# A planned mLSTM and top-1 expert kernel: paced row stores, two joined lead tiles, a shorter selection and a new order

## The chip, the cores and the metric

The kernel runs on one core of one Trainium2 chip. The metric is device time in microseconds of one execution, and the time of a kernel is the median of its runs.

## The reference, cut to what matters

An mLSTM recurrence over 768 steps, for 4 batches and 8 heads of width 40, gives 3072 tokens of 320 numbers. Each token goes to the one expert of eight that its gate picks, and the expert's two-layer product is scaled by the gate's probability.

```python
for t in range(S):                                   # B, H, S, D = 4, 8, 768, 40
    m_new = np.maximum(f_gate[:, :, t] + m, i_gate[:, :, t])
    f_stab, i_stab = np.exp(f_gate[:, :, t] + m - m_new), np.exp(i_gate[:, :, t] - m_new)
    C = f_stab * C + i_stab * einsum('bhd,bhe->bhde', vt, kt)
    n = f_stab * n + i_stab * kt
    y[:, :, t] = sigmoid(o_gate) * einsum('bhde,bhe->bhd', C, qt) / max(abs(n . qt), 1)
...
x = y.transpose(0, 2, 1, 3).reshape(3072, 320)
logits = x @ w_gate + modality_bias[modality_id]     # 8 experts
e_idx = argmax(logits); gate_w = softmax(logits)[e_idx]
for e in range(8):
    out[e_idx == e] = gate_w * (maximum(x @ w1[e], 0) @ w2[e])   # w1 320x1024, w2 1024x320
```

## The kernel before, in words

**What runs.** `still_arm` (from L1654) is the arm that these inputs take. It treats the recurrence's state as settled after the first 64 steps of each batch, so a chunk of 128 tokens is one set of products of queries with a state (`light`, L1955; `light16`, L1979; `special`, L2070). There are 24 chunks. `token_rows` (L1996) divides, gates and splits two chunks at a time into 16-bit rows in the tile `rows`; the dividing multiply of a pair of chunks runs on GpSimd (L2027), the split on ScalarE (L2029) and VectorE (L2031).

**From chunks to expert tiles.** Tokens are sorted by modality, because with this bias almost all tokens of a modality choose the same expert: class A and class B. Each chunk's 128 rows are stored to their sorted places in the DRAM tensor `x_s` by an indirect transfer that GpSimd issues (`scatter_rows`, L2035). Two transfers of `prefill` (L2050, issued on SyncE by L2054 and L2055) first fill parts of `x_s` with empty rows, and every row store waits for them. SyncE fetches an expert tile of 256 rows back, transposed, once the chunks that can hold its rows have landed (`load_tile`, L2120). The first three tiles of class A do not go through DRAM: `select` (L2142) multiplies rows of a chunk by a 0/1 matrix and so gets the transposed tile in PSUM. These lead tiles are A0 with 128 rows, from chunks 0 to 2; A1 with 64 rows, from chunks 1 to 3; and A2 with 128 rows, from chunks 2 to 5. Each chunk of a selection is five matmuls (L2158), two half ones (L2161) and two products of one column each (L2163) that bring the token's number in two parts into one PSUM column.

**The expert.** `expert` (L2221) first forms the hidden layer of a tile, eight blocks of 128 hidden units, each from six full matmuls (L2255) and from half-height ones for the last 64 inputs (L2263). ScalarE applies the ReLU (L2243), VectorE forms the remainder (L2244), and 24 matmuls for each 128 rows give the output (L2295). A part of 64 rows does them in pairs. ScalarE scales the output (L2310) and GpSimd scatters it to `out` (L2311).

**What sets the order.** Nothing is issued in the order of the source. Every piece of work is a task with an engine, a duration and what it reads and writes. `Plan.run` (L65) is a list scheduler: of the tasks that are ready on an engine it takes the one with the least latest time plus a nudge, one letter of the string `PRIO` for each task, (character code − 79) × 0.5. Each transfer has a second letter, in `LOADS`, which shifts by the same rule the moment from which it may be planned; the letters stand in the order in which the transfers are declared, and those of `prefill` are the 14th and 15th. The instructions are then written to each engine's queue in the order of the planned starts, and each engine works through its queue in order. For each gap of TensorE in the plan's first 60, `emit` (L2485) puts in idle matmuls on zeros (L2494).

**Limits around GpSimd.** `swdma` (L1680) makes every GpSimd transfer wait for the completion of the last but one before it. `Plan.run` keeps tasks marked `port` from overlapping, since GpSimd and some VectorE operations share a port.

Of the kernel before, what the change touches and what calls it, by code (L numbers as in the profile page):

```python
# [21 lines left out]
class Plan:  # L22
# [151 lines left out]
P = 128  # L174
# [42 lines left out]
def kernel(  # L217
# [1346 lines left out]
LEAD = {"A0": (0, 3), "A1": (1, 4), "A2": (2, 6)}  # L1564
STREAM = ["A0", "A1", "A2", "B0", "B1", "A3", "B2", "A4", "B3", "A5", "B4", "A6", "B5", "A7"]
# [6 lines left out]
    "+i&.3%&&nIL8]tk*G%<-YU4cr2-I{Q]G'%E)%g+%Q%3dK`7M_D%p%%R22j%SS;J05Cj+-]I{&K*)99Lz{n%{f[Ut%)^OI&UT{2f'(R2lf-KAaB"  # L1572
    "22%=%vwLleYz]{%N-,B8CBT%{%0/(%k>+%qM%T^[8(%i,%,t5OAt4;h@/{T.%>,t'=+m>@dSV4i@91)^/%l,&%DfAmT&*L;P5(B%%%+sO&Z0Ez"
    "{nc_pkYo%A)\\vk8T]M5)Zy]EEq\\y{%P*/KZ2JV%/QhvP9GRL3>/-bPCSSa%QL9>.jW)JI,-2lkA{+%5-Q4=&_>%{%';J%MrK-K,%gnRmh/-/^%"
    "%%B%%+(VXI',s:'4.%/g%S%0=9'r9\\SG%9-EPfl{Y4w]DB\\&8Q+s%W7^,Sr%dWl/%mkW@>%%%%%%(9F?(V(%Tkhk\\{YHP*n_5v23ep&%1cl=HU"
    "n%bV]%MjlD'[e%\\4*%%&%,E?(@%x*\\Ts'N0.{\\Wsy'{;/qif{.Qod48%%{*%qD5k,R,UBn9'\\c1'KEr))%\\@(%d%%%%?(,&%%)%[/VWns5<Z[D"
    "euy[_s{@X26)uk?Is'O/.W%>aH%%%1n?J'mr/'7?)<'E^6-%%*%%,B%%%%8%F7(x-<*dCmC%[dZCD4P5v+2&-@GE%+@t%RL.-&'%.r%7)\\g/']"
    "^%@''S/'%%;%%%E(11%%%%7)*4'007W{Q%dw2bFX;M:bFR%Q2,t7m%Rx:@1%.%g%0'Ur/,'j/C'6rB?%%,%%%H05.%%1%@OO4%vUs<*HcIM'\\z"
    "bN*neWM/)M2B)BP{/Y%ip%-L:7k6-BJRI)HY1%/%83b.ns%K'D_22%0%%%%uF%%%%%%:AUb<4=<{\\%cai\\^VP,4%+/(*`/%h%g,+]%/6?%%%8<"
    "M(2%D:%%;(C{QxNtE3H'1?S[%x<03V@92+{{'hh)*8{1_%%6:,%F5^l&lSKmKD7kiTs/{xAt6%W'46Yr0%GB0'oli1'c\\3&%%%1%/\\(%%*%%0A"  # L1580
    ",9HN*6%7'%c/Q%R:M'kO3'%%%%%&A(B'%%%%M(',vrt@'tL.'H[JS%;:=+%%%'B%?(&%:%)%;93(K&@r/F_T7,rRrb'R%/'%%%%%%D(%%%%%%5"
# [63 lines left out]
def still_arm(tc, a, out):  # L1645
# [10 lines left out]
    def pe(dur, fn, r=(), w=(), **k):  # L1656
        plan.add("PE", dur, fn, r, w, **k)
# [32 lines left out]
    sws = []  # L1690
# [345 lines left out]
    def scatter_rows(c):  # L2036
        def scatter():
# [9 lines left out]
    scats = {}  # L2047
# [589 lines left out]
```

## Time and profile before

| what | value |
| --- | --- |
| median of 3 runs | 223.42 us (222.77, 223.42, 224.87) |
| the profiled execution's own time | 225.65 us |
| span of the profiled execution | 223.8 us, so 1.85 us lie around it |
| TensorE busy | 212.5 us, 95% of the span |
| VectorE, ScalarE, GpSimd busy | 139.0, 99.2, 75.6 us |
| mean granted TensorE clock | 0.986 of full speed |
| DMA | 30.77 MB, mean 137 GB/s |

The busy time of TensorE contains the idle matmuls on zeros and whatever ran at a lower clock, so a busy TensorE is not the same as useful work. The parts of the page that matter most here are the slices of the span, where the granted clock and the DMA share stand under each other, and the chain of work that ended last, which goes through TensorE for most of its length.

### The profile page before, as it was taken

Reading aid. Unit: us, or ns where it says so; the run is one execution under the profiler, and the core shown is the slowest. Engines: PE = TensorE matmul, PEld = TensorE weight load, DVE = VectorE, ACT = ScalarE, POOL = GpSimd, SP = SyncE. Lnnn points to the kernel's source line nnn. Section 1 sums busy time; section 2 is a strip of 40 time slices with the busy share of each in tenths; the row PEclk is TensorE's granted clock in tenths of the full one; section 3 lists DMA queues with packets and bytes.
Section 4 is the critical chain, followed back from the end, with each engine's and each line's share of the span. In section 5 each row is a group of like instructions: output and inputs, shape, how many; then the busy total and the mean of one; then the engine's idle time right before and its main releaser. Section 6 shows DMA issues by size and latency. Waiting matters only on the chain.

```text
span 223.8 us, 5532 instructions
## 1 busy us (share of the span) xinstructions
PE 212.5 (95%) x2180; PEld 160.6 (72%) x2182; DVE 139.0 (62%) x446; ACT 99.2 (44%) x202; POOL 75.6 (34%) x84
## 2 busy tenths in 40 slices
PE   8998997999999999899999999999999999999790
PEld 3665785897877777677777787777777877777550
DVE  7987765469795895989428149346831770449800
ACT  2497766385645814774336033234235321313220
POOL 5122228224535264552452126552511103111031
PEclk9999999699999999999999999999999999999997
DMA  6999879457262621755414410240191100691010
GB/s 190 357 309 398 288 203 305 186 127 253 80 166 93 146 106 61 191 150 90 149 59 104 152 62 0 106 113 11 62 237 14 46 3 29 153 378 62 3 39 21
DMA packets 27115, 30.77 MB, mean 137 GB/s; under 512 B 19190, under 2 KB 19480, under 8 KB 26824
## 3 DMA queue, kind: packets, MB, share of 16 engines
q1 hardware_dynamic: 24520, 22.06, 33.2%
q0 software_dynamic: 2416, 8.13, 10.7%
q8 instruction: 19, 0.31, 0.6%
q10 hardware_dynamic: 144, 0.13, 0.2%
q14 instruction: 16, 0.13, 0.2%
HBM read 18.57 MB, written 8.22 MB: 120 GB/s over the span
## 4 chain that ended last, share of the span: by engine, by line
PE 65%; issue 18%; DMA 5%; DVE 4%; POOL 3%; SPq 1%; POOLq 1%; ACT 0%; ACTq 0%
PE O L2295 24%; PE H L2255 21%; PE H L2263 6%; PE M L2494 3%; DMA qg<-in_ql 3%; PE Y L1969 3%; POOL out L2311 3%; DMA out<-ob,ois 2%; SPq L1941 1%; PE M L2195 1%; PE Y L2094 1%; PE Y L2079 1%; PE O L2158 1%; DVE ql L1977 1%; DVE hl L2244 1%
## 5 line engine op out<-in xcount | busy, mean ns | idle before, releaser
L2244 DVE SCALAR_TENSOR_TENSOR hl<-H,hh 128x512 f16<-128x512 f32 (+1 forms) x52 | 33.6, 656 | 29.8 <-ACT hh L2243 25.9
L2243 ACT ACTIVATE hh<-H 128x512 f16<-128x512 f32 (+1 forms) x52 | 29.4, 571 | 51.4 <-PE H L2263 30.9
L2295 PEld LDWEIGHTS <-hh 128*128 128x128 f16 (+1 forms) x400 | 38.4, 99 | 14.4 <-ACT w2hB L1942 0.2
L2311 POOL DMA_INDIRECT out<-ob,ois x25 | 25.5, 1019 | 66.8 <-ACT ob L2310 36.6
L2255 PE MATMUL H<-xt,w1hA 128*128 128x256 f16 (+2 forms) x256 | 36.3, 252 | 0.9 <-issue 0.9
L2038 POOL DMA_INDIRECT x_s<-rows,pos_i x24 | 24.1, 1006 | 32.0 <-DVE hl L2244 7.9
L2255 PE MATMUL H<-xt,w1hB 128*128 128x256 f16 x192 | 32.9, 273 | 0.0
L2255 PE MATMUL H<-xt,w1lA 128*128 128x256 f16 (+2 forms) x128 | 29.9, 252 | 0.5 <-issue 0.5
L2310 ACT ACTIVATE ob<-O,zs 128x320 f32<-128x320 f32 x24 | 12.5, 525 | 38.2 <-PE O L2295 19.9
L2295 PE MATMUL O<-w2hA,hh 128*128 128x320 f16 (+1 forms) x104 | 28.1, 304 | 0.0
L2295 PE MATMUL O<-w2lA,hh 128*128 128x320 f16 (+1 forms) x104 | 28.1, 304 | 0.0
L2295 PE MATMUL O<-w2lB,hh 128*128 128x320 f16 x96 | 26.4, 299 | 0.0
L2295 PE MATMUL O<-w2hB,hh 128*128 128x320 f16 x96 | 26.4, 299 | 0.0
L2255 PE MATMUL H<-xt,w1lB 128*128 128x256 f16 x96 | 26.2, 272 | 0.0
L2255 PEld LDWEIGHTS <-w1hA 128*128 128x128 f16 x256 | 21.0, 99 | 6.0 <-issue 3.7
L2295 PEld LDWEIGHTS <-hl 128*128 128x128 f16 (+1 forms) x200 | 19.2, 98 | 7.9 <-issue 0.5
L2027 POOL TENSOR_TENSOR xr<-xr,ab 128x640 f32<-128x640 f32 x11 | 14.9, 1358 | 25.7 <-DVE ab L2010 19.9
L2255 PEld LDWEIGHTS <-w1hB 128*128 128x128 f16 x192 | 17.4, 98 | 4.2 <-issue 2.1
L2295 PE MATMUL O<-w2hA,hl 128*128 128x320 f16 (+1 forms) x104 | 15.9, 299 | 0.0
L2012 DVE SCALAR_TENSOR_TENSOR xr<-og,Y 128x320 f32<-128x320 f32 x24 | 11.3, 477 | 7.3 <-PE Y L2094 4.9
L2295 PE MATMUL O<-w2hB,hl 128*128 128x320 f16 x96 | 15.0, 299 | 0.0
L2494 PE MATMUL M<-zz 128*128 128x512 bf16 (+7 forms) x46 | 12.9, 427 | 1.3 <-DVE zz L1785 1.1
(205 smaller groups left out, 344.0 us busy)
## 6 DMA issues: line engine op xcount, KB each, us to landing
qg<-in_ql SPq DMA_DIRECT2D x11, 384.0 KB
og<-in_ogl SPq DMA_DIRECT2D x12, 320.0 KB
stage<-in_w1s SPq DMA_DIRECT2D x8, 320.0 KB
stage<-in_w SPq DMA_DIRECT2D x8, 320.0 KB
stage<-in_w1t SPq DMA_DIRECT2D x1, 1280.0 KB
og<-in_w SPq DMA_DIRECT2D x1, 1280.0 KB
kvs<-in_kvs SPq DMA_DIRECT2D x2, 364.5 KB
sp<-in_spq SPq DMA_DIRECT2D x4, 160.0 KB
```

The costliest lines, as they stand in the source:

```text
L1969: t_.matmul(y[p0:p1, HQ * g:HQ * g + w], lhsT=q[0:k, i, g, p0:p1], rhs=Ss[b][0:k, g, 0:w], start=(g == 0), stop=(g == 2), skip_group_check ...
L2012: dve(320, lambda h=h: v.scalar_tensor_tensor(x4[:, h], og[k][:, h].rearrange("p (h d) -> p h d", h=H), 1.0, y4[h][:, :, 0:D], ALU.add, AL ...
L2027: pool(640, lambda: g_.tensor_tensor(x3, x3, ab.rearrange("p c h o -> p (c h) o").broadcast_to([P, 2 * H, D]), ALU.mult), r=abk, w=xk)
L2038: ins = g_.indirect_dma_start(out=x_s[:, :], out_offset=bass.IndirectOffsetOnAxis(ap=pos_i[:, c:c + 1].bitcast(U32), axis=0), in_=rows[:, ...
L2243: act(g * n, lambda: s_.activation(hh[:, sl, 0:n], hp3, AF.Relu), r=[nb], w=[f"hh{j}{i}" for i in fs])
L2244: dve(g * n, lambda: v.scalar_tensor_tensor(hl[:, sl, 0:n], hp3, 0.0, hh[:, sl, 0:n], ALU.max, ALU.subtract), r=[nb] + [f"hh{j}{i}" for i ...
L2255: t_.matmul(dst, lhsT=w[:, i, ws], rhs=x[:, xb], start=(first and b == 0 and q == 0), stop=(last and b == 1 and q == 2), skip_group_check= ...
L2263: t_.matmul(dst, lhsT=w[rs, place(f)[0], 2 * T:WP], rhs=x[rs, xs[r]], start=(first and r == 1 and m == 0 and q == 0), stop=(m == len(pairs ...
L2295: t_.matmul(op[p0:p0 + nr, 0:DM], lhsT=t[:, at[f], P * h:P * h + nr], rhs=w[:, f], start=(i < ways), stop=(i >= 24 - ways), skip_group_che ...
L2310: act(400, lambda op=op, o=o, qc=qc, nr=nr: s_.mul(obs[o][0:nr], op[0:nr, 0:DM], facs[0:nr, qc:qc + 1]), r=[no, f"fac{k}"], w=[f"ob{o}"])
L2311: swdma(164, lambda o=o, qc=qc, nr=nr: disjoint("outf", g_.indirect_dma_start(out=out[:, :], out_offset=bass.IndirectOffsetOnAxis(ap=ois[0 ...
L2494: t_.matmul(bank[b][:, 0:m], lhsT=zz, rhs=zz[:, 0:1].broadcast_to([P, m]), start=True, stop=True, skip_group_check=True)
```

## The change

Four things change together.

1. GpSimd's transfers no longer wait for the last but one before them. In the plan, any GpSimd transfer that would start before `UNTIL` is moved to at least `GAP` after the one before. In the program, a chunk's row store that the plan starts before `UNTIL` waits for the last VectorE instruction that the plan has ended by then.
2. Tiles A1 and A2 get one buffer, side by side, and one pass through `expert`: the hidden layer of 192 columns at once, then the output of the 64 rows and of the 128 rows.
3. A chunk of a selection brings both parts of the token's number by one matmul of two columns; VectorE adds the two when it copies them.
4. `PRIO` and `LOADS` are new strings (`PRIO`, eleven lines of letters, is left out below).

```diff
+    GAP = 2.4
+    UNTIL = 48.0
...
+        last_sw = -100.0
...
             if t["port"]:
                 s = max(s, port_free)
+                if t["kb"] is not None:
+                    s = max(s, last_sw + self.GAP) if s < self.UNTIL else s
+                    last_sw = s
                 port_free = s + t["dur"]
...
+JOINT = ("A1", "A2")
...
 LOADS = (
-    "7%D.4%V6%%K7{t{0^+cV]6:%3n^>{{b)>4RR;I2+,{Clb%4{q.%00QeG/'g+0i@={7du*T%B%y?8FY(B9..'fSaVV+/MH{&%?Bf5((D%Df%Z,["
+    '(1%@7KO:%.5-{jlT=%.%,M%CeJOgFm&tuM%IN3`uGP1G<+{W0GN%+Dh%8{2nLGa%Su7c_%zC2b7%,DH)ZX4Jy<I0UKIn%^%@B=2NfjjcHge<1I'
...
     def swdma(kb, fn, r=(), w=(), **k):
-        def go():
-            ins = fn()
-            if len(sws) > 1:
-                tc.add_manual_dep(ins.ins, sws[-2].ins.name, mybir.DependencyInfo(mybir.DependencyClass.Sync, mybir.DependencyReason.DATA),
-                                  reason="two of GpSimd's transfers under way")
-            sws.append(ins)
-
-        plan.add("POOL", 1.05, go, r, w, kb=kb, port=True, **k)
+        plan.add("POOL", 1.05, fn, r, w, kb=kb, port=True, **k)
...
             scats[c] = ins
+            if pace:
+                tc.add_manual_dep(ins.ins, pace[-1].ins.name, mybir.DependencyInfo(mybir.DependencyClass.Sync, mybir.DependencyReason.DATA),
+                                  reason="transfers of rows follow one another at the plan's distance")
...
+        if name in JOINT:
+            at = TILES[name][0] - TILES[JOINT[0]][0]
+            j0, nj = STREAM.index(JOINT[0]) % SLOTS, sum(TILES[m][1] for m in JOINT)
+            whole = xt[j0][:, 0:6 * nj].rearrange("p (b n) -> p b n", b=6)
+            x = whole[:, :, at:at + n]
...
-                for w in range(2):
-                    t_.matmul(o1[0:n, ib:ib + 1], lhsT=sel, rhs=tok2[:, c, w:w + 1], start=False, stop=z_ and w == 1, skip_group_check=True)
+                t_.matmul(o1[0:n, ib:ib + 2], lhsT=sel, rhs=tok2[:, c], start=False, stop=z_, skip_group_check=True)
...
-            dve(1, lambda: v.tensor_copy(ids[0:n, q:q + 1], o1[0:n, ib:ib + 1]), r=[n1_, "ids_z"], w=[f"ids{k}"])
+            dve(2, lambda: v.tensor_scalar(ids[0:n, q:q + 1], o1[0:n, ib:ib + 1], o1[0:n, ib + 1:ib + 2], None, ALU.add), r=[n1_, "ids_z"], w=[f"ids{k}"])
...
     def expert(k):
         s = slots[k]
+        if s["name"] in JOINT[1:]:
+            return
+        subs = [m for m in range(len(STREAM)) if STREAM[m] in JOINT] if s["name"] in JOINT else [k]
+        c, n, x = s["cls"], s.get("nj", s["n"]), s.get("whole", s["x"])
...
-        sets = [(0, 1), (2, 3), (4, 5), (6, 7)] if n == T or by_piece else [(0, 1, 4, 5), (2, 3, 6, 7)]
+        sets = [(0, 1), (2, 3), (4, 5), (6, 7)] if n > P or by_piece else [(0, 1, 4, 5), (2, 3, 6, 7)]
...
+        t = plan.tasks[i]
+        pace.clear()
+        if t["w"] and t["w"][0][:2] == "xs" and plan.start[i] < plan.UNTIL:
+            pace.extend([max((z, n, x) for n, (z, x) in enumerate(steps) if z <= plan.start[i])[2]])
+        made = t["fn"]()
+        if t["eng"] == "DVE" and hasattr(made, "ins"):
+            steps.append((plan.end[i], made))
```

## Rows read from the trace of the kernel before

**Rows 1.** The page, busy time of each engine, share of the span, instructions

```profile
PE 212.5 (95%) x2180; PEld 160.6 (72%) x2182; DVE 139.0 (62%) x446; ACT 99.2 (44%) x202; POOL 75.6 (34%) x84
```

**Rows 2.** Idle matmuls of L2494 by stretch: us, PE and weight loads busy, clock, DMA, GB/s

```profile
0.00:24.00 24.00, 14.16 (x51) 5.11 (x53) 1.00 0.91 319
```

**Rows 3.** Timeline of PE: start, length, what, and the idle time before it

```profile
21.34 0.87 PE L1969 MATMUL Y<-S,qg 120*128 120x123 f32 x6 [0.55 <-DMA qg<-in_ql]
```

**Rows 4.** The chain of waits, in order of time: start, length, what

```profile
37.01 0.53 PE H L2255 x18
37.54 0.39 issue
...
38.15 0.52 issue
...
38.86 0.52 issue
...
39.63 0.46 PE H L2263 x24
```

**Rows 5.** Stretches: us, busy PE, PEld, DVE, ACT, POOL (instructions), clock, DMA, GB/s

```profile
38.00:39.00 1.00, 0.34 (x3) 0.06 (x3) 0.00 (x0) 0.00 (x0) 0.98 (x2) 1.00 0.99 397
...
40.00:50.00 10.00, 10.00 (x156) 8.88 (x150) 6.45 (x22) 6.36 (x14) 1.86 (x2) 0.83 0.48 135
```

**Rows 6.** Timeline of POOL: the first and the fifth row store

```profile
32.14 1.18 POOL L2038 DMA_INDIRECT x_s<-rows,pos_i  x1 [4.84 <-DVE w1lB L1943]
...
37.46 0.97 POOL L2038 DMA_INDIRECT x_s<-rows,pos_i  x1 [0.30 <-issue]
```

**Rows 7.** The page, the DMA queue of instructions with most packets: packets, MB, share

```profile
q8 instruction: 19, 0.31, 0.6%
```

**Rows 8.** The line of the number products, all instructions: ns min, median, max

```profile
L2163 PE MATMUL O<-cst,sel x20: 163/170/178, 14.6 to 32.5; 128*128 128x1 f16 x14, 128*64 128x1 f16 x6
```

**Rows 9.** The chain of waits at number products and an idle matmul

```profile
22.80 0.80 PE M L2494 x4
...
28.52 0.13 PE O L2163 x2
```

**Rows 10.** The chain of waits at hidden layers, of 128 and then of 256 columns

```profile
45.14 1.45 PE H L2255 x24
46.59 0.78 PE H L2263 x24
...
68.61 1.31 PE H L2255 x12
69.92 0.76 PE H L2263 x12
```

**Rows 11.** What POOL waited for: us in total, times, longest

```profile
POOL x_s L2038 <- DMA out<-ob,ois: 3.2, 2, 2.7
```

**Rows 12.** Timeline of SyncE's queue: filler rows of `x_s`, B0's load

```profile
18.51 0.98 SPq L2054 DMA_DIRECT2D x_s<-zrow  x1
...
28.39 0.61 SPq L2055 DMA_DIRECT2D x_s<-zrow  x1
...
43.61 1.46 SPq L2126 DMA_TRANSPOSE xt<-x_s  x1
```

**Rows 13.** Stretches: DMA share ahead of the row stores and behind B0's load

```profile
28.00:32.00 4.00, 4.00 (x58) 3.45 (x55) 3.50 (x9) 2.20 (x4) 0.00 (x0) 1.00 0.63 154
...
47.00:48.00 1.00, 1.00 (x23) 0.90 (x18) 0.89 (x2) 0.66 (x3) 0.00 (x0) 1.00 0.66 259
48.00:49.00 1.00, 1.00 (x18) 1.00 (x17) 0.97 (x2) 1.00 (x2) 0.24 (x1) 1.00 0.09 27
```

**Rows 14.** Timeline of PE: B0's first matmuls

```profile
54.07 0.38 PE L2255 MATMUL H<-xt,w1hB 128*128 128x256 f16 x2
```

**Rows 15.** Timeline of DVE and of ACT: rows of chunks 4, 5 and A2's last copy

```profile
28.57 0.88 DVE L2031 TENSOR_TENSOR rows<-xr,rows 128x128 f16<-128x128 f32 x2
...
35.38 0.37 ACT L2172 CAST xt<-O 128x256 f16<-128x256 f32 x1
```

**Rows 16.** Timeline of POOL: the last output store

```profile
218.74 0.97 POOL L2311 DMA_INDIRECT out<-ob,ois  x1 [1.83 <-ACT ob L2310]
```

More of the change, by code (lines that the diff above doesn't have):

```diff
@@ L1571 @@
 PRIO = (
[L1572 to L1581, printed above, removed]
@@ L1582 @@
-    "(,%xjr>'CCD'pMO:-R>))+A%%%R7%%3*%%%_("
+    "{r&(,%u6*7PG+X<;_Zu]mk{3Z{3,&d'.-4-+2{{utsf0/KK%%@%Sm75{zg%(\\bj5hg1^eRl7K\\_JHTRSQ'fKMs+;7%s{{P4+WLGnKREzPNM{[P"
+    "Z%T5s.1(aVd[SUN{D9*3+&/*+PvUHV8LM;{%&ENRM;63)oW%%%'*;D.ZUrHNW_Npt-%fW_RQ_?xOe_K%.Z4Q3O+Rs.73E2N%1[\\X_[WO*5eSAq"
+    'L1PYU6P%?%5fi4gsDyWJIF8M{7^IH`Wp&%r()50A%%(%4%=4%%k{OOk9/%Z%/%;0>??1ITWGcy{U%VZ[fSGDGHswuS40.10HP2SmwqDBn.P,Qd'
+    '`y][t;FX%u(&%2%(%%0%%8T-%)%%BA>2HJ=6L[@c?)%{;%WVEC%+946[EXzzxT\\WzWXzswQOY]F^mtpoxmq_@%kXlidH{%Y%r%%%<):@MC&MMY'
@@ new lines @@
+    "Vzi%'BMfwGQE-?vCs{,YT%%%%%{X?3zpur{bo_{{z%{%[yoIEz%DiiLTdt{urZw]imwTm_fu\\OdbbRRYRtsr<xLKIFE`%/%%%+%9QHfsyoz{1Q"
+    "Nzm3yI>UT^VQJ2%NE{rt{QjI`y'fp`dc`]aM+oy.)l2'xD%x\\YroW=Eq{r%)B%%c[{w{h\\{{W{mnE5WXUeSE/(KHEASPnQjWyh4@m4HEEaPIBy"
+    "=>@M<:x/310**(d3I%%%J{&%I_dd`^K`{{z@J%*%')%F''%%%uuP/(L6Qk.3Md1*jKEh+{b'F30:8o%-,)(&:E,+I%+*{pvk-PB{],o{_`4Vsq"
+    "OS]jSyH{O*{,-wcceH^Qc=U`yHv'4P6yq,jJ:R7,_7MGs2IVT>V,&MC8PNSg%%Q%fehW@a4e%*%f1C7PMwL1JnqAGEWNIGjLD2)'%';3%'03%0"
+    "0%+Q.+cce)%et_cbq%%A?uvtsNv*Qh{O:1(U'm]C%DvI]9>DC@@zs00-fd,*naXQTg%%<(*+ET0+6&*7bAJ4*:y7'%@(9*%D%B?24\\c-%5E3:{"
@@ L1583 @@
+    "y*1N`),2sk0+K]3%-&'%ZE%*%@%%0>[i@''\\dCIKY,4.,B<*RS,))%><3%.%97.'*%%%/:7M;`J8,&,5'0*5*,&.%*%3;*.9975*(*%%)+KI5["
+    "G1,&/,@0.+',&/-'%(%%',%%%))2%"
 )
 LOADS = (
-    "7%D.4%V6%%K7{t{0^+cV]6:%3n^>{{b)>4RR;I2+,{Clb%4{q.%00QeG/'g+0i@={7du*T%B%y?8FY(B9..'fSaVV+/MH{&%?Bf5((D%Df%Z,["
-    '?2X\\k%)4]%VLN{,`[-y@'
+    '(1%@7KO:%.5-{jlT=%.%,M%CeJOgFm&tuM%IN3`uGP1G<+{W0GN%+Dh%8{2nLGa%Su7c_%zC2b7%,DH)ZX4Jy<I0UKIn%^%@B=2NfjjcHge<1I'
+    'AjB%%/5NT4L:DC]X{6%W'
 )
@@ L2105, in tile_rows @@
         hs = halves(name)
-        slots[k] = dict(name=name, cls=name[0], n=n, hs=hs, nh=len(hs), r0=r0, need=need, x=xt[j][:, 0:6 * n].rearrange("p (b n) -> p b n", b=6), s=j,
-                        q=slice(hs[0][0], hs[0][0] + len(hs)))
+        x = xt[j][:, 0:6 * n].rearrange("p (b n) -> p b n", b=6)
+        if name in JOINT:
[3 more added lines that the diff above has]
+            x = whole[:, :, at:at + n]
+        slots[k] = dict(name=name, cls=name[0], n=n, hs=hs, nh=len(hs), r0=r0, need=need, x=x, s=j, q=slice(hs[0][0], hs[0][0] + len(hs)))
+        if name == JOINT[0]:
+            slots[k].update(whole=whole, nj=nj)
     def behind(ins, need):
@@ L2222, in expert @@
         s = slots[k]
-        nh, c, n = s["nh"], s["cls"], s["n"]
+        if s["name"] in JOINT[1:]:
+            return
+        subs = [m for m in range(len(STREAM)) if STREAM[m] in JOINT] if s["name"] in JOINT else [k]
+        c, n, x = s["cls"], s.get("nj", s["n"]), s.get("whole", s["x"])
         w1h, w1l, w2h, w2l = W[c]
-        x = s["x"]
         j = k % 2
         hh, hl = hhs[j], hls[j]
-        xk = [f"x{s['s']}"] + ([f"xb{s['s']}"] if f"xb{s['s']}" in plan.writer else [])
+        xk = [f"x{slots[m]['s']}" for m in subs]
+        xk += [f"xb{slots[m]['s']}" for m in subs if f"xb{slots[m]['s']}" in plan.writer]
         one = max(n / 256 * 0.109 + 0.001, 0.031)
         by_piece = k in ALONE
-        sets = [(0, 1), (2, 3), (4, 5), (6, 7)] if n == T or by_piece else [(0, 1, 4, 5), (2, 3, 6, 7)]
+        sets = [(0, 1), (2, 3), (4, 5), (6, 7)] if n > P or by_piece else [(0, 1, 4, 5), (2, 3, 6, 7)]
         g = len(sets[0])
-        xc = [f"xc{s['s']}"]
+        xc = [f"xc{slots[m]['s']}" for m in subs]
         if s["name"] not in LEAD:
@@ L2285, in expert @@
             finish(fb, nb, h3[1])
-        for h, (qc, _, nr) in enumerate(s["hs"]):
+        for h, (m_, qc, o_, nr) in enumerate((m, qc, r - s["r0"], nr) for m in subs for qc, r, nr in slots[m]["hs"]):
             no, op = take("O")
@@ L2290, in expert, with mm @@
             for q in range(0, 24, 4):
-                def mm(q=q, h=h, op=op, nr=nr, ways=ways):
+                def mm(q=q, o_=o_, op=op, nr=nr, ways=ways):
                     for i in range(q, q + 4):
@@ L2294, in mm @@
                         p0 = 64 * (i % ways)
-                        t_.matmul(op[p0:p0 + nr, 0:DM], lhsT=t[:, at[f], P * h:P * h + nr], rhs=w[:, f], start=(i < ways), stop=(i >= 24 - ways),
+                        t_.matmul(op[p0:p0 + nr, 0:DM], lhsT=t[:, at[f], o_:o_ + nr], rhs=w[:, f], start=(i < ways), stop=(i >= 24 - ways),
                                   skip_group_check=True)
@@ L2495, in emit @@
                 n -= m
-        plan.tasks[i]["fn"]()
+        t = plan.tasks[i]
[5 more added lines that the diff above has]
+            steps.append((plan.end[i], made))
     cut = order.index(found["cut"])
```

13 lines of the change are left out of this document (6 added, 7 removed).

## The prediction

> **What bounds the kernel now.** I read the busy times first, then the idle matmuls, then the chain of waits, then short stretches around its holes. TensorE is busy for 212.5 of 223.8 us [rows 1]; the reader is to see that no other engine comes near. But 14.16 us of that are idle matmuls, all in the first 24 us [rows 2], when inputs are still arriving. From there on time is lost only where TensorE stops, where its clock is low, or where its work is longer than it need be.
>
> The chain has one bad place. A1's hidden layer, 64 columns wide, runs 18 matmuls in 0.53 us and then three times stands still, 0.39, 0.52 and 0.52 us, 1.43 in all [rows 4]. Those waits are "issue": nothing that the profile shows was awaited. In the middle of it TensorE is busy for 0.34 of a microsecond, VectorE and ScalarE not at all, and the DMA engines for 0.99 [rows 5]. GpSimd's first five row stores start from 32.14 to 37.46 us [rows 6], just ahead. Then the clock falls: over 40 to 50 us it is 0.83 of full on average although TensorE is busy all the time, with its two levels of 2.4 and 1.2 GHz [rows 5]. That loses 10 x 0.17 = 1.7 us.
>
> My reading is that TensorE ran out of instructions: they come by DMA too, through a queue of their own [rows 7], the small matmuls use them up fastest here, and the transfers had filled the DMA engines. The row of the stall does not prove this.
>
> **The change part by part.** The profiled execution took 225.65 us, its span of 223.8 and 1.85 around it. It stands 2.23 above the median of 223.42.
>
> *Number products.* Ten chunks of selections have two each, 20 in all [rows 8]; a pair of 128 rows takes 0.13 us of the chain [rows 9], so one of the two is 0.065. The three of A0 come before the last idle matmuls, which start at 22.80 [rows 9] and would only grow: nothing. A2's four save 4 x 0.065 = 0.26. A1's three have 64 columns and the same latency of 170 ns; I count them at a quarter, 0.04 in all, since their pairs overlap the matmuls beside them. Sum 0.3; the bounds are 0, if TensorE waits for rows there anyway, and 7 x 0.065 = 0.46. The added second operand on VectorE's copy costs nothing, because TensorE has other work in that stretch; without that cover it is one small operation's length.
>
> *Joined tiles.* A1 alone: 48 full matmuls at 0.53/18 = 29 ns are 1.41 us, and 24 half ones 0.46, so 1.87 [rows 4]. A2 alone: 24 full ones take 1.45, so 48 take 2.90, and the half ones 0.78: 3.68 [rows 10]. Together 5.55. No row has 192 columns. Between 128 columns (60 ns each) and 256 (1.31/12 = 109 ns) the line gives 85 ns, so 48 x 85 = 4.07; the half ones lie between 0.78 and 2 x 0.76 = 1.52, so 1.15. Sum 5.22: 0.33 saved. Scaled from the 256 row alone it is 0.75 x (4 x 1.31 + 1.52) = 5.07, so 0.48; scaled from the 128 row alone 1.5 x 3.68 = 5.52, so 0.03. I take the line, which uses the nearest row on either side. The output matmuls stay as many. ScalarE and VectorE evaluate as many elements in four pieces as before; they are off the chain here.
>
> *The stall.* The 64-column burst is gone, and by the new letters the stores can leave their bunch. I take the 1.43 us [rows 4] as saved in full, between 0 and 1.43, and the clock loss with it. For the clock the profiled run shows 1.7 us [rows 5], but the three timed runs differ by 2.1 us, about what having or not having that loss would make. Their median lies 0.65 above the fastest, so I count 0.65 against the median, between 0 and 1.7.
>
> *Removed waits.* GpSimd lost 3.2 us in two places to the rule of two transfers [rows 11]. It is busy for 75.6 of 223.8 us [rows 1], so I count nothing; its idle time covers it. If a row store behind such a wait is late for its tile, the cover is gone, and up to 3.2 us come back as a gain.
>
> *Added waits.* Each paced store holds GpSimd's queue until its VectorE instruction is done. Behind it wait the next store and the dividing multiply of the next two chunks, for which ScalarE and VectorE wait. The cadence was (37.46 - 32.14)/4 = 1.33 us [rows 6]; at the plan's 2.4 the fifth store comes 4 x 1.07 = 4.28 later if the first stays where it was. SyncE's load of B0 waits for the fifth: it was issued at 43.61 [rows 12] and DMA had gone quiet by 48 to 49 [rows 13]; B0's first matmul was at 54.07 [rows 14]. So some 6 us of cover, of which an earlier TensorE takes away 0.3 + 0.33 + 1.43 + 0.65 = 2.7. The rest, 3.4, is 0.9 short of 4.28. Against that stands that the first store can start earlier. The two transfers that fill `x_s` with empty rows have to precede every store. The first was issued at 18.51, exactly its old letter's shift ('t', 18.5); the second had '{', 22, and went out at 28.39 [rows 12]. Their new letters are 'j' and 'l', 13.5 and 14.5. Between 28 and 32 us DMA was busy for 0.63 only [rows 13], so there is room for stores ahead of the crowd. I take 0, and keep 0.9 of idle time, with a clock loss of 1.7 behind it, as the other end.
>
> *New order.* The letters decide what each queue does next, and no row shows the new one. What it could win is bounded by the head: at 21.34 TensorE had waited 0.55 us for queries, ran a chunk of 0.87 that A0 does not need, and spent 0.80 on idle matmuls at 22.80 [rows 3, 9], 2.2 us together. It could lose as much if another load is late. I take 0. The tail, whose last store begins at 218.74 behind ScalarE's copy [rows 16], is the same work.
>
> *The sum.* 0.3 + 0.33 + 1.43 + 0.65 = 2.7 against the median, so 220.7. With the clock loss in full it is 3.76: 221.9 against the profiled execution's own time, 219.7 against the median. I forecast 220.2, the middle of 219.7 and 220.7.
>
> **Rivals.**
> *The stall stays or moves.* If TensorE stops for another reason, or the code of the joined tile comes as late, only 0.3 + 0.33 are saved: 222.8. For it: the row names no cause, and more stores may now overlap. Against: the stall ends in the middle of a group of six matmuls on the same inputs, which no data explains. In the Trainium skill, "Runtime: NRT & Kernel Launch", section "Instruction fetch mechanics", code is fetched in 16 KiB blocks by a queue of the engine's own and crossing a block is mostly hidden; by that rule fetching did not cause the stall, and this rival's 222.8 would be the result. The trace neither confirms nor refutes it: it has such packets and a stall without a named cause.
>
> *Pacing makes B0 late (slower).* Place: GpSimd's queue between the fifth store and SyncE's load of B0. If the VectorE instruction that opens the first store ends 3 us after 32.14, B0 lands about 48 + 4.28 + 3 = 55.3, while TensorE wants it at 54.07 - 2.7 = 51.4: 3.9 us idle, and 1.7 for the clock. 223.42 - 2.7 + 5.6 = 226.3. It decides for slower once the first store starts about 2.6 us later than before (at 2.6 the result is 225.9). For it: the fifth store's margin is already negative at the old start. Against: the earlier letters of the empty rows.
>
> *The joined tile waits.* It cannot start before A2's last copy, 35.38 + 0.37 = 35.75 us, which A1 alone did not need; the cover to 37.01, where A1's first stretch runs, is 1.3 us [rows 4, 15]. If rows of chunks 4 and 5, written from 28.57 on [rows 15], come 2.5 us later, TensorE idles 1.2 and loses 1.7 for the clock: 223.42 - 2.7 + 2.9 = 223.6, no change.
>
> *The head is shortened too.* The 2.2 us of A0's start come on top: 218.0.
>
> **How the numbers follow.** Chances: forecast 0.44, head shortened 0.11, stall stays 0.20, joined tile waits 0.11, pacing late 0.14. One per cent of 223.42 is 2.23, about what a measurement of this kernel can tell from no change: faster is below 221.19, slower above 225.65. The forecast's own range is 219.4 to 221.2; the low end has the head's gain in it, the high end the shorter delays of the pacing case. Leaving out part of the head case and the worst of the pacing case gives 217.8 to 224.9. Faster: 0.43 + 0.11 = 0.54. Same: 0.01 + 0.20 + 0.09 of waiting joined tiles = 0.30. Slower: 0.14 + 0.02 = 0.16.
>
> **What would show it.** Right: no "issue" piece on the chain between 35 and 45 us, clock 1.00 from 40 to 50, stores about 2.4 us apart beginning before 32, 10 number products instead of 20, and a joined hidden layer of about 5.2 us. Wrong: an idle place of TensorE ahead of the joined tile or of B0, named by a transfer or a copy; a low clock in another stretch; the same stall with the stores apart, which would clear the DMA engines of it.

## The result, and the profile after

The changed kernel takes **225.08 us** (median of 20 runs) against 224.37 us for the kernel before in as many runs beside it: a ratio of **1.006, interval 1.0033 to 1.0087**. Timed twice more it gave 1.0024 (0.9993 to 1.0054) and 1.0023 (0.9995 to 1.0052). So it is not faster: the first interval lies above 1, the other two contain it, and all stay within the 1% that I called no change. The forecast was 220.2 us, with a range of 217.8 to 224.9. (Where a line number in the prose above differs by a few from the printed functions, the printed one holds.)

The profiled execution took 227.37 us, its span 225.3. It is longer than the others, which took 223.71 to 226.53 us but for one of 425.72, and the ratio leaves both out; what is read from it below is held against two later profiles. First the page, then the idle matmuls of the head, the number products and SyncE's queue (columns as in [rows 1, 2, 8, 12]).

```profile
PE 213.2 (95%) x2100; PEld 159.2 (71%) x2103; DVE 138.6 (61%) x446; ACT 101.0 (45%) x202; POOL 75.3 (33%) x84
```

```profile
0.00:24.00 24.00, 13.04 (x48) 5.03 (x51) 1.00 0.91 312
```

```profile
L2170 PE MATMUL O<-cst,sel x10: 170/177/178, 14.9 to 32.4; 128*128 128x2 f16 x7, 128*64 128x2 f16 x3
```

```profile
22.94 0.48 SPq L2056 DMA_DIRECT2D x_s<-zrow  x1
...
42.26 1.46 SPq L2134 DMA_TRANSPOSE xt<-x_s  x1
```

TensorE has 80 instructions fewer but no less busy time. The number products are ten instead of twenty, the second store of empty rows goes out at 22.94 instead of 28.39, and B0's load at 42.26 instead of 43.61. The chain of waits shows the joined tile, and behind it the surprise (columns as in [rows 4]).

```profile
38.05 0.50 PE H L2265 x6
...
39.38 0.60 PE H L2265 x6
39.98 0.60 PE H L2273 x12
40.58 2.09 PE H L2265 x24
42.67 0.60 PE H L2273 x12
43.27 1.10 PE H L2265 x12
44.37 0.39 PE O L2305 x4
...
46.26 3.40 PE O L2305 x32
...
50.29 1.63 PE O L2305 x12
...
73.01 0.57 PE Y L1988 x18
73.58 0.54 PE H L2273 x8
74.12 0.95 issue
75.07 0.38 PE H L2273 x3
75.45 0.38 issue
75.83 0.28 PE H L2273
76.11 0.43 issue
76.54 2.64 PE H L2265 x12
```

The place of the old stall is clean. The same picture now stands at 74.12 to 76.54: a run of short matmuls (18 light ones in 0.57 us), and then three stops without a named cause, 1.76 us in all, where [rows 4] had 1.43. The stretches (columns as in [rows 5]) show that the clock loss went with it.

```profile
40.00:50.00 10.00, 10.00 (x113) 7.99 (x114) 9.86 (x23) 7.76 (x17) 4.04 (x4) 1.00 0.60 181
...
72.00:73.00 1.00, 1.00 (x12) 0.72 (x11) 0.29 (x1) 0.37 (x2) 0.93 (x1) 1.00 0.98 191
74.00:75.00 1.00, 0.12 (x4) 0.00 (x0) 0.21 (x1) 0.00 (x0) 0.69 (x2) 1.00 0.67 230
76.00:80.00 4.00, 3.57 (x17) 2.35 (x17) 2.38 (x5) 1.35 (x3) 2.82 (x3) 0.59 0.18 65
```

Where [rows 5] read 0.83 over 40 to 50 us it is 1.00; from 76 to 80 it is 0.59, mostly at the lower level of 1.2 GHz, behind TensorE's stop. GpSimd's timeline shows the paced row stores, the bunch of transfers ahead of the new stop, and the end.

```profile
29.75 1.21 POOL L2036 DMA_INDIRECT x_s<-rows,pos_i  x1 [1.58 <-DVE w2lA L1941]
...
39.51 0.97 POOL L2036 DMA_INDIRECT x_s<-rows,pos_i  x1 [1.03 <-issue]
...
69.30 0.94 POOL L2321 DMA_INDIRECT out<-ob,ois  x1 [0.80 <-ACT og L1947]
70.55 1.21 POOL L2321 DMA_INDIRECT out<-ob,ois  x1 [0.30 <-DVE zs L2218]
72.07 0.97 POOL L2036 DMA_INDIRECT x_s<-rows,pos_i  x1 [0.30 <-issue]
73.34 0.97 POOL L2321 DMA_INDIRECT out<-ob,ois  x1 [0.30 <-issue]
74.62 0.97 POOL L2321 DMA_INDIRECT out<-ob,ois  x1 [0.30 <-issue]
...
217.87 0.97 POOL L2321 DMA_INDIRECT out<-ob,ois  x1 [2.29 <-ACT ob L2320]
219.15 0.90 POOL L2381 DMA_INDIRECT out<-sp,fo_i  x1 [0.31 <-issue]
```

The first and the fifth row store are 9.76 us apart (5.32 in [rows 6]); from 69.30 on five transfers follow one another 1.25 to 1.52 us apart. At the end the order of two things has turned. The verdict word (`bword`) says whether this arm's assumptions hold; at the end every engine loads it and branches over the other arm. The odd row is the one token at most whose expert is not that of its modality; VectorE computes it apart, and it has a store of its own. In the changed kernel the odd row's store comes last, and so does TensorE's product for the verdict word, as its timeline and VectorE's copy of the word show.

```profile
52.65 0.38 PE L2265 MATMUL H<-xt,w1hB 128*128 128x256 f16 x2
...
217.54 0.18 PE L2420 MATMUL M<-bsum,ones 128*128 128x1 bf16 x1
217.76 0.16 DVE L2422 CAST bword<-M 128x1 int32<-128x1 f32 x1 [5.94 <-PE M L2420]
```

TensorE ends at 217.72, the span at 225.3: **7.6 us of tail** behind TensorE's last matmul, against 217.85 to 223.8, or 5.95, before. Two later profiles of the changed kernel have 7.45 and 7.65. The records of single instructions hold branches and waits that the views leave out. By them all engines read the verdict word from 217.94 on and take their branch at 218.49 to 218.98; the next instruction comes at 222.64 on ScalarE, 222.69 on VectorE, 222.92 on SyncE, and already at 219.09 on TensorE. Before, SyncE and VectorE had gone on behind their branch by 215.2, ScalarE branched at 218.49 and went on at 220.99, and GpSimd, through its branch at 219.60, waited for its last store to land until 221.80. Around the span there are 2.0 to 2.1 us in the median of the changed kernel's runs and 1.75 to 1.8 before.

One gain was not in the forecast. Before, TensorE waited once near the end for VectorE, which was busy with the odd row (timeline of PE, kernel before):

```profile
208.37 0.38 PE L2263 MATMUL H<-xt,w1hA 64*128 64x256 f16 x3 [1.30 <-DVE hl L2244]
```

Both profiles of the kernel before have it (1.30, 1.36 us); none of the three profiles of the changed kernel has it.

### The profile page after: what moved, and what is told of

The parts are those of the page before. It is cut to its first block, busy times and chain, and to the rows that moved or that the text cites. A ratio compares the mean times of both kernels' runs of the same rounds, so it can differ in the third digit from the quotient of the medians.

```text
span 225.3 us, 5384 instructions
## 1 busy us (share of the span) xinstructions
PE 213.2 (95%) x2100; PEld 159.2 (71%) x2103; DVE 138.6 (61%) x446; ACT 101.0 (45%) x202; POOL 75.3 (33%) x84
## 4 chain that ended last, share of the span: by engine, by line
PE 53%; issue 25%; POOL 6%; DMA 6%; ACT 3%; SPq 2%; DVE 2%; POOLq 1%; ACTq 0%
PE O L2305 22%; PE H L2265 18%; PE H L2273 5%; POOL out L2321 4%; DMA stage<-in_w 4%; DMA og<-in_ogl 2%; PE Y L1988 2%; PE Y L1967 2%; POOLq L1685 1%; PE M L2202 1%; PE Y L2080 1%; PE O L2166 1%; SPq L1939 1%; ACT og L1947 1%; ACT rows L2027 1%
## 5 line engine op out<-in xcount | busy, mean ns | idle before, releaser
L2254 DVE SCALAR_TENSOR_TENSOR hl<-H,hh 128x512 f16<-128x512 f32 (+2 forms) x52 | 33.9, 656 | 35.0 <-ACT hh L2253 33.2
L2253 ACT ACTIVATE hh<-H 128x512 f16<-128x512 f32 (+2 forms) x52 | 29.4, 572 | 48.9 <-PE H L2273 29.6
L2321 POOL DMA_INDIRECT out<-ob,ois x25 | 24.9, 997 | 72.2 <-ACT ob L2320 61.0
L2265 PE MATMUL H<-xt,w1hA 128*128 128x256 f16 (+2 forms) x224 | 34.9, 262 | 0.0
L2265 PE MATMUL H<-xt,w1hB 128*128 128x256 f16 x192 | 33.6, 278 | 0.4 <-issue 0.4
L2265 PE MATMUL H<-xt,w1lA 128*128 128x256 f16 (+2 forms) x112 | 28.7, 261 | 0.0
L2265 PEld LDWEIGHTS <-w1hA 128*128 128x128 f16 x224 | 19.6, 98 | 4.4 <-issue 2.2
L2305 PE MATMUL O<-w2hB,hl 128*128 128x320 f16 x96 | 15.8, 299 | 0.0
L2025 POOL TENSOR_TENSOR xr<-xr,ab 128x640 f32<-128x640 f32 x11 | 14.0, 1275 | 4.9 <-DVE ab L2008 4.8
L2504 PE MATMUL M<-zz 128*128 128x512 bf16 (+8 forms) x49 | 13.3, 411 | 1.2 <-DVE zz L1783 1.1
```

What stands on the lines that cost most here:

```text
L2025: pool(640, lambda: g_.tensor_tensor(x3, x3, ab.rearrange("p c h o -> p (c h) o").broadcast_to([P, 2 * H, D]), ALU.mult), r=abk, w=xk)
L2253: act(g * n, lambda: s_.activation(hh[:, sl, 0:n], hp3, AF.Relu), r=[nb], w=[f"hh{j}{i}" for i in fs])
L2254: dve(g * n, lambda: v.scalar_tensor_tensor(hl[:, sl, 0:n], hp3, 0.0, hh[:, sl, 0:n], ALU.max, ALU.subtract), r=[nb] + [f"hh{j}{i}" for i ...
L2265: t_.matmul(dst, lhsT=w[:, i, ws], rhs=x[:, xb], start=(first and b == 0 and q == 0), stop=(last and b == 1 and q == 2), skip_group_check= ...
L2305: t_.matmul(op[p0:p0 + nr, 0:DM], lhsT=t[:, at[f], o_:o_ + nr], rhs=w[:, f], start=(i < ways), stop=(i >= 24 - ways), skip_group_check=True)
L2321: swdma(164, lambda o=o, qc=qc, nr=nr: disjoint("outf", g_.indirect_dma_start(out=out[:, :], out_offset=bass.IndirectOffsetOnAxis(ap=ois[0 ...
```

## The experiments

**Theories.** T: the late verdict word and the odd row's late store cost the end what the saved work gives. S: the stop has only moved, from 37 to 74 us. For the stop itself: C, a boundary of a block of TensorE's code falls behind a run of short matmuls; B, GpSimd's bunched transfers make it alone.

### Both kernels again

No edit.

> The changed kernel unaltered, for its time beside the kernel before and for a second profile. In the first profile TensorE's last matmul ends as early as before (217.7 us against 217.9) although the hole at 37 to 44 us is gone; a new hole of 1.76 us with a clock loss of 1.7 us stands at 74 to 80 us, behind five GpSimd transfers 1.3 us apart, and the span ends 7.6 us behind the last matmul, before 6.0. Theory A (late verdict): the end is longer by about 1.6 us in every execution, because the branch that all engines take waits for a word that TensorE now forms last. Theory B (bunched transfers): the hole at 74 us is there in every execution too, with or without the clock loss. Rival: the hole belongs to that one execution and the head is what is slower. Time expected 224.5 to 225.5, 1.002 to 1.010 of before.

> The kernel before unaltered, for a second profile. The runs of before beside the first comparison had a mean clock of 0.994 to 0.999 in most executions and 0.988 to 0.991 in the others, which were 1.5 to 2.5 us longer, so the profile that the prediction was read from (0.986) looks like one of the longer kind. Theory: in the usual execution the three waits of about 0.5 us at 37 to 39 us are there or shorter, but no stretch at half clock follows; the end behind the last matmul is 6.0 us as in the first profile. Rival: the waits themselves are absent too, and the forecast gain had nothing to come from. Time as the other runs of before, ratio 1.00.

After: 223.75 us, 1.0024 (0.9993 to 1.0054). Its stop of 1.07 us is at 72.7 to 75.05, without a low clock, and TensorE ends at 214.14, the span at 221.6. Before: 223.88, 1.0005 (0.9967 to 1.0042), with its stop of 1.24 us at 40.1 to 41.9. The clock behind that stop is 1.00 over 40 to 50 us; the low clock of this execution stands at 22 to 28 us, in the head. So the stop belongs to each kernel at its own place, and the clock loss behind it does not come every time: I had read it from one profile.

### The verdict word early

```diff
-    plan.nudge(PRIO, LOADS)
+    plan.nudge(PRIO, LOADS); [t.update(nudge=-60.0) for t in plan.tasks if t["eng"] == "PE" and "bsum" in t["r"]]
```

> The changed kernel with one letter's weight altered: TensorE's product for the verdict word (one matmul of one column) is planned as soon as its operand is there, instead of behind the last output matmul. Theory A: the engines other than TensorE have taken their branch before the last output is stored, so the end behind the last matmul is 6.0 to 6.5 us instead of 7.6 and the time falls by 1.1 to 1.6 us, to about 223.6. Rival (the last store's landing sets the end, the branch is hidden under it): no change, within 0.3 us.

230.55 us, 1.031 (1.0268 to 1.0353), but for a reason beside the question. One task's nudge changed, and the planner put VectorE's work on the odd row, which waits for a 1.3 MB load, ahead of a remainder `hl` of the tile under way:

```profile
196.83 0.58 PE L2273 MATMUL H<-xt,w1hB 64*128 64x256 f16 x3 [5.57 <-DVE hl L2254]
```

With the odd row's product early as well (the same edit for `facc`):

> As the one before, and the odd row's product planned early too, so that its store no longer follows the last output store. Theory A: the last store is now the output's, begun at 217.9 instead of 219.15, so another 0.3 to 1.2 us fall away: 222.6 to 223.4. Rival: the end is set by the branch alone, or TensorE loses as much waiting for the odd row's operand: no further gain.

229.82 us, 1.031 (1.0273 to 1.0346), with 4.69 us of the same wait. So the times say nothing about the end, but the tails do: 6.38 and 6.32 us. The runs also show how steep the order is: one nudge costs 5.6 us of TensorE here. The next runs therefore move tasks in the finished order and leave every other place as it is.

### The two late products moved, and the reverse

```diff
+    order = _moved(plan, order, found, ...)   # product and copy of the verdict word (and the odd row's, with its store)
     cut = order.index(found["cut"])           # set ahead of the last tile's output matmuls; or, in the kernel before, behind everything
```

> The changed kernel in its own order, with two instructions alone moved in their queues: TensorE's product for the verdict word goes ahead of the last tile's output matmuls and VectorE's copy of it ahead of its last remainder. Theory A (late verdict): engines that are done take the branch early, so the end behind the last matmul shrinks from 7.5 to about 6 us and the time falls by 0.9 to 1.5 us, from 1.002 to about 0.997 of before. Rival (the last store's landing, begun at 219.15 in the first profile, sets the end): within 0.3 us of the changed kernel.

> As the one before, and the odd row's product, its copy and its store also moved ahead of the last tile's output. Theory A with the odd row: the last store is the output's and begins 1.3 us earlier than the odd row's did, so a further 0.3 to 1.0 us: 0.993 to 0.996 of before. Rival: the odd row's small store was hidden under the branch's code or under the landing of the output's store: no further gain, or a loss of up to 0.7 us for its 0.7 us on TensorE if the operand is late.

> The kernel before in its own order, with the verdict word's product and copy alone moved behind the last output matmul, where the changed kernel has them. Theory A: the end behind the last matmul grows from 6.0 to about 7.5 us, 1.004 to 1.007 of before. Rival: nothing, 1.000, since in this kernel the output's last store decides.

Verdict moved: 224.88 us, 1.0036 (1.0 to 1.0072), tail 6.33. Both moved: 223.47 us, **1.001** (0.9973 to 1.0046), tail 6.35. The verdict made late in the kernel before: 224.90 us, **1.0074** (1.0033 to 1.0114), tail 6.88 in place of 5.95 and 5.7. The two moves gained less than I expected (0.997, and 0.993 to 0.996), and their intervals overlap those of the changed kernel. GpSimd's last store in the second and in the third of these:

```profile
217.21 0.97 POOL L2321 DMA_INDIRECT out<-ob,ois  x1 [2.24 <-ACT ob L2320]
```

```profile
217.25 0.97 POOL L2311 DMA_INDIRECT out<-ob,ois  x1 [1.83 <-ACT ob L2310]
```

Both follow TensorE's end by 0.9 us, as before; in the changed kernel it is 1.43, since the odd row's store stands behind. From the start of the last output store to the span's end there are 5.07 us before, 5.46 with both moved and 6.00 with the verdict late.

In the tail the late word is shown in both directions; in time it is shown by the kernel before alone, with 1.0074. The odd row's store has no share in the tail, which is as long with the word moved alone. Two things take longer with the late word, and the runs do not tell which of them sets the end. One is the way from an engine's branch to its next instruction: with the late word in the kernel before, and in the changed kernel, it takes 3.78 and 4.16 us on ScalarE and 3.95 and 4.11 on VectorE, against 2.50 and 3.15 before and 2.67 and 3.10 with both moved. The other is the landing of the last store: 3.97 us behind its start with the late word, 3.03 and 2.81 in the two profiles of the kernel before.

What the moves leave of the longer tail, some 0.4 to 0.6 us, is on GpSimd. Its own branch takes 2.69 us with both moved, and the store has landed by then; before it took 0.51, and GpSimd then waited for the store. The 0.2 us around the span stay with both moved as well (1.99 in the median).

### The rule of two transfers, back and away

```diff
# in the changed kernel: the wait of swdma put back; in the kernel before:
-            if len(sws) > 1:
+            if False:
```

> The changed kernel with the old rule put back in the program alone: each GpSimd transfer waits for the last but one before it; order and pacing as in the changed kernel. Theory B: the five transfers of 69 to 75 us move apart, the hole at 74 us closes or shrinks, and the time falls by 0.5 to 1.8 us. Rival: the rule only lets GpSimd wait, the hole stays or GpSimd's queue gets late for the chunks: no change or up to 1 us slower.

> The kernel before without the rule of two GpSimd transfers under way, and nothing else. By my term of the sum: no change (0; the cover is GpSimd's idle time), and 3.2 us less waiting of GpSimd. If the rule holds transfers apart that otherwise starve TensorE: a longer stop at 37 to 41 us, or a new one between 60 and 110 us, and 0.5 to 2 us more than before.

Back: 224.15 us, 1.0047 (1.0023 to 1.0071). The stop at 74 is gone; the changed kernel and the two runs with a nudge, timed beside it, all had it. GpSimd's transfers start at 69.22, 72.09, 73.36 and 76.14 here, farther apart. In its place TensorE waits for results of VectorE and ScalarE, which the timeline names, so nothing is gained:

```profile
79.57 0.21 PE L1997 MATMUL Y<-Sh,qh 120*128 120x123 f16 x1 [0.63 <-DVE xr L2019]
...
91.73 0.31 PE L2314 MATMUL O<-w2hA,hh 128*128 128x320 f16 x1 [0.34 <-ACT hh L2262]
...
93.19 0.31 PE L2314 MATMUL O<-w2hA,hh 128*128 128x320 f16 x1 [0.74 <-ACT hh L2262]
```

Away: 221.17 us, 1.0015 (0.9992 to 1.0038). My term for the rule, nothing, lies within this interval, but so does a loss of up to 0.8 us, and the trace shows where one may be: GpSimd's branch takes 2.41 us, the tail is 6.42 (5.94 in the kernel before with the number product alone, of the same series), and 1.98 us lie around the span in the median, against 1.81.

### The blocks of code shifted

```diff
-                m = min(n, 512)
+                m = min(n, 256)
```

> The idle matmuls of the first 24 us are cut into pieces of at most 256 columns instead of 512: the same columns, some 48 more TensorE instructions, so that every boundary of a 16 KB code block falls some 50 to 100 instructions earlier in the program. Theory C (the stop at 72.7 to 76.5 us comes when a block boundary falls behind a run of short matmuls while transfers fill the DMA engines): the boundary moves from behind the 64-column work at 73 us to about 70.5 to 72, and the stop of 1.1 to 1.8 us there is gone or is moved with it; if it is gone, 222.8 to 224.0 us, 1 to 1.5 below the changed kernel. Theory B (GpSimd's transfers 1.3 us apart make it alone): the stop stays at 73 to 76 us, with its length, and the time stays within 0.3 of the changed kernel's.

> The same edit in the kernel before, whose stop of 1.2 to 1.4 us stood at 37 to 41 us in three profiles. Theory C: no stop at 37 to 41 us (the boundary moves to about 34 to 36, where the work is sparse), a new one possibly at 45.5 to 47, where the next boundary falls among short matmuls; 221.8 to 223.0 us if no new one comes, against 223.4 to 223.9 before. Theory B: the stop stays at 37 to 41 us and the time does not change (223.4 to 223.9).

> The changed kernel with both late products, their copies and the odd row's store moved ahead of the last tile's output, and with the idle matmuls cut at 256 columns. Theory C: the 0.6 to 1.2 us of the end and the stop at 73 us are both saved, 221.5 to 222.8 us, below both kernels. Theory B: the end's gain alone, 223.0 to 224.0.

The 16 KB packets of the instruction queue did move: in the kernel before they now go out at 32.85 and 43.19 us, in the changed one at 69.32. The stops did not. Chain of waits of the kernel before with the edit:

```profile
37.50 0.16 PE H L2263 x3
37.66 0.41 issue
38.07 0.23 PE H L2263 x3
38.30 0.51 issue
38.81 0.25 PE H L2263 x5
39.06 0.51 issue
39.57 0.37 PE H L2263 x13
```

The lengths are those of [rows 4] within 0.02 us, the place within 0.2. The changed kernel stops for 1.05 us at 73.7 to 75.4, and for 1.55 at 72.6 to 75.0 with the late products moved. Theory C falls. Times: 224.32 us, 1.0034 (0.9996 to 1.0073); before 222.26, **0.9938** (0.9906 to 0.9971); moved 223.12, 0.9987 (0.995 to 1.0025). The gain of the second, 1.4 us, is not in the stop; its wait for VectorE near the end is 0.57 us instead of 1.30, and where the rest comes from no run shows.

### Without pacing

```diff
-            pace.extend([max(...)[2]])
+            [].extend([max(...)[2]])
```

> The changed kernel without the waits that hold its first six row stores back for VectorE (the order stays as it is, so the stores go when their rows are ready). If pacing costs time on GpSimd's queue: 0.3 to 1 us less than the changed kernel. If pacing keeps TensorE's code and rows from being late: a stop of about 1 us comes back between 30 and 45 us and the time is 1 us longer. If it does neither: the same within 0.3 us, which I expect, since B0's first matmul did not come later than before (52.65 against 54.07).

225.02 us, 1.0053 (1.0015 to 1.0092). The first five row stores now run from 27.73 to 33.61, B0's first matmul is at 52.95 (52.65 with pacing), and TensorE waits 0.74 us at 34.75 to 36.2 between A0's outputs. The stop at 74.0 to 76.5 is there with 2.03 us. Pacing neither costs nor gains a time that can be told here.

### Transfers or burst, and the number product alone

```diff
# few rows: the joined tile's and B0's stores
+            nr = 8 if s["name"] in ("A1", "B0") else nr
# burst later: the 18 light matmuls moved behind the third group of B0's outputs, in the finished order
# number alone, in the kernel before
-                for w in range(2):
-                    t_.matmul(o1[0:n, ib:ib + 1], lhsT=sel, rhs=tok2[:, c, w:w + 1], ...)
+                t_.matmul(o1[0:n, ib:ib + 2], lhsT=sel, rhs=tok2[:, c], ...)
```

> The changed kernel with both late products moved ahead (223.47 us, a stop of 1.48 us at 73 to 76 us), in which the output stores of the joined tile and of B0, four of the five GpSimd transfers between 69 and 75 us, store 8 rows each instead of up to 128: the rest of those output rows is left out. The instructions, their order and TensorE's work stay. If the bytes of these transfers starve TensorE: no stop at 72 to 77 us, no low clock behind it, and 221.5 to 222.5 us. If the burst of 18 short matmuls makes the stop by itself: the stop stays at 1 to 1.8 us, and 223.0 to 224.0 us.

> The same changed kernel with the late products ahead; the 18 short light matmuls at 73 us (and VectorE's first reading of them) are moved behind the third group of B0's output matmuls that follow, some 3 to 4 us later; GpSimd's transfers stay. If transfers alone make the stop: it stays at 73 to 76 us with 1 to 1.8 us, 223.0 to 224.0 us. If the burst alone makes it: it moves behind the burst, to about 76.5 to 78, with its length, same time. If it needs both: no stop at either place, 222.0 to 222.8 us.

> The kernel before with one number product per chunk of a selection in place of two, and the sum of the two columns on VectorE; its order, its tiles and its waits stay. By my term of the sum: 0.3 us less (0 to 0.46), so 0.9986 of before, hardly to be told from no change. A rival: ten instructions fewer shift everything that follows and the time moves by up to 1 us either way, as cutting the idle matmuls alone did (0.9938).

220.79 us, 0.9995 (0.9972 to 1.0017); 220.89 us, 1.0004 (0.9983 to 1.0025); 220.43 us, **0.9972** (0.9946 to 0.9998). The first two have both late products moved ahead, and neither has a stop. But nothing follows from that, because in these runs, and in the one without the rule above, no kernel stopped: the kernel before took 220.94 us beside them, against 223.0 to 224.4 in all other series. The mean granted clock is not the difference: in the median it was 0.995 for the kernel before there, and 0.994 to 0.996 elsewhere. This is the chain of the kernel before with the number product alone, where all others have the stop:

```profile
36.34 0.70 PE H L2254 x24
37.04 0.46 PE H L2262 x24
37.50 0.81 PE H L2254 x24
...
39.13 1.75 PE O L2294 x24
...
45.37 0.54 PE O L2294 x4
...
46.55 2.72 PE O L2294 x20
```

A1's hidden layer runs through in 1.97 us. GpSimd's transfers are as close there as ever (DMA share in this run and in the one without the rule, columns as in [rows 5]):

```profile
35.00:38.00 3.00, 3.00 (x78) 2.56 (x77) 1.22 (x6) 1.98 (x5) 2.39 (x3) 1.00 0.97 344
```

```profile
38.00:41.00 3.00, 3.00 (x76) 2.62 (x72) 1.73 (x6) 2.17 (x5) 2.52 (x4) 1.00 0.97 380
```

So full DMA engines and a run of short matmuls, together, do not suffice. Theory B falls too as it was put.

### The last two

> The changed kernel, unchanged, for the third time. If it runs where the stops show (before about 223.4 to 224.4 us): 1.002 to 1.007 of before, with a stop at 73 to 76 us. If it runs where they do not (before about 221 us): the work that is saved on TensorE (0.3 for number products, 0.3 to 0.4 for the joined hidden layer) against 0.7 more in the output matmuls and 1.4 to 1.8 at the end: 1.0 to 1.9 us slower, 1.004 to 1.008. A rival: the end's cost is hidden there as well, 0.998 to 1.002.

> The kernel before with one number product per chunk of a selection and with the idle matmuls cut at 256 columns; its order, tiles and waits stay. Alone the first gave 0.9972 and the second 0.9938, on different days' chips. If both gains are real and add up: 0.990 to 0.995 of before. If the second was only a lucky shift of the odd row's weights against the last tile: 0.995 to 0.999.

After: 223.41 us, 1.0023 (0.9995 to 1.0052), with its stop of 1.29 us at 73.3 to 75.6 and a tail of 7.65. The two gains together: 222.37 us, 0.9978 (0.994 to 1.0017); the stop at 37 to 39 is there with 1.39 us. They do not add up to the 0.990 to 0.995 that I expected if both were real, and no version has a ratio below 0.9938.

## Why the prediction was wrong

**Two steps failed.** In size the larger is the stall, "I take the 1.43 us [rows 4] as saved in full, between 0 and 1.43, and the clock loss with it": with 0.65 for the clock that is most of the 2.7 us. The three profiles of the changed kernel have a stop at 73 to 76 us instead, of 1.76, 1.07 and 1.29 us. The other is the last sentence on the new order: "The tail ... is the same work."

**The tail** is the same work in another order, and I took that as free. The trace of before had what I needed: it shows TensorE's end, and 5.95 us behind it in which only the branch on the verdict word and the last store run. I never asked what the new letters do to those two. They put the word's product and the odd row's store last, and the tail grew by 1.5 to 1.9 us. With the word moved back 1.1 to 1.3 of that are gone; making the word late in the kernel before gave 1.0074. The other 0.4 to 0.6, and 0.2 around the span, are not the word's: they stay with both moved back, and the kernel before without the rule of two transfers has them too. By the Trainium skill, "Runtime: NRT & Kernel Launch", section "Instruction fetch mechanics", a taken branch to code that is not at hand waits for a fetch; the trace agrees, with more packets of the instruction queues behind the branch in the changed kernel (8 of one queue after 216 us, 4 before).

**The stall** was saved where it stood, and another came at 74 us. That was my rival "stays or moves", which I gave 0.20; its 222.8 us are 0.997 of before, and with both late products back the ratio was 1.001 (0.9973 to 1.0046). No block boundary makes the stop: shifting the blocks left it where it was. That agrees with the section of the Trainium skill that I set against my reading in the prediction, by which crossing a block is mostly hidden. My reading, that the crowded DMA engines starve TensorE of instructions, is not shown either: two profiles at a DMA share of 0.97 have no stop.

**The clock loss** of 0.65, and 1.7 in full, was counted from one profile and three runs. In the two profiles of the kernel before, the stop stood once with a low clock behind it and once without; in the three of the changed kernel, once with and twice without. It was counted as a gain of the change, but it hangs on the stop, which stayed.

**The price of both** may have been right in size. In the series without stops the kernel before took 220.94 us, 2.1 to 3.4 less than elsewhere, and the prediction's stall and clock loss come to 2.1 to 3.1; but what else differed there is not known. In that series the changed order with the late products moved back, and the light matmuls later, takes as long as the kernel before (1.0004, 0.9983 to 1.0025): without the stops and the late word the rest of the change comes to nothing.

**Joined tiles.** The sum had 5.22 us for the hidden layer; the chain gives 0.50 + 0.60 + 0.60 + 2.09 + 0.60 + 1.10 = 5.49, so 0.06 saved of the 0.33. A matmul of 192 columns takes 4.29/48 = 89 ns, not 85. The two tiles apart were taken at 5.55, with A1 at 1.87; without a stop A1 takes 1.97, so 0.16 are saved. But "the output matmuls stay as many" hid a loss: they take 0.39 + 3.40 + 1.63 = 5.42 us, against 1.75 + 0.54 + 2.72 = 5.01 for the two tiles apart. The joined tile costs about 0.25 instead of saving 0.33.

**Number products**: right in sum, partly by luck. The starts on TensorE put 0.92 us on them before and 0.64 after. Of these 0.28 us A0's products have 0.08, which the forecast rightly left out; A2's save 0.10, not 0.26, and A1's 0.10, not 0.04. So 0.20 where 0.3 was forecast. Alone they gave 0.9972, 0.6 us with an interval of 0.04 to 1.2.

**Added waits**: right. The fifth store came 2.05 us later (39.51 against 37.46), but the first came 2.4 earlier, and B0 started at 52.65 instead of 54.07 [rows 14]. The rival of late B0 did not happen. **Removed waits**: counted as nothing, for GpSimd's idle time; the runs leave room for a loss of up to 0.8 us, and the trace has 0.4 to 0.6 of it at the end, where GpSimd is not idle. **New order**: my bound of 2.2 us either way was right as a size by luck, since it was taken from the head, and what was won and lost lies near the end: 1.3 us of the wait for VectorE won, the tail lost.

**The sum as measured**: -0.2 for the products, +0.25 for the joined tile, about 0 for the stall and the clock, -1.3 for VectorE, +1.7 to 2.1 for the end: +0.45 to 0.85 us. The ratio of 1.006 is 1.3 us, those of 1.0024 and 1.0023 are 0.5. The wait for VectorE and the joined tile are read from profiles; no run changed either alone.

**Left open**: what makes the stop. It has the same place in each kernel, follows a run of short matmuls while GpSimd's transfers are close, is not tied to code blocks, was gone when the rule moved the transfers apart (one profile), and was absent from all four kernels profiled in one series. What was different in that series no row shows, and whether the recording of the profile has a part in the stop no run can tell.

## What to carry to other kernels

Read the end of a kernel as a stage of its own: what decides the last branch or the last store must be computed before the last big piece of work, and a new order has to be read for it. A stall without a named cause may be counted as moved, not as saved, until an experiment removes it. A loss that one profile shows is worth its share of the runs that have it, and joining two tiles has to be priced with everything behind the join, its outputs too.

## What the runs showed of the hardware

- The stop comes in steps. TensorE resumes every 0.71 to 0.76 us (38.07, 38.81, 39.57; 75.07, 75.83, 76.54), does one to six matmuls and stops again; a stop has two to four such pieces.
- The kernel before took 0.9 to 1.5% less time in one series of runs than in the others (220.94 us against 223.0 to 224.4), and the four kernels profiled in that series have no stop.
- How long an engine takes from a branch to its next instruction depends on the engine and on what else runs. In the seven profiles in which all five branch together at the end, SyncE takes 3.4 to 4.4 us, VectorE 3.9 to 4.3, ScalarE 2.9 to 4.2 and TensorE 0.55. Branching apart, VectorE takes 2.9 to 3.2, ScalarE 2.45 to 2.9 and TensorE 0.07; SyncE takes 2.55 to 2.75 where the late products are moved ahead, but 5.5 in the kernel before, where it branches alone at 193.5 us and the DMA share is 1.01 from 196 to 200.
